# DeltaNet attention and a PReLU feed-forward on one NeuronCore: the triangular systems of the first two chunks solved by factors, and more weight staging

## The chip, the cores and the metric

The kernel runs on one core of one Trainium2 chip. A core has five engines with instruction streams of their own: TensorE (PE: matrix products, with a separate step that loads the stationary operand, PEld), VectorE (DVE), ScalarE (ACT), GpSimd (POOL) and SyncE (SP), which here only issues DMAs. Products land in PSUM, eight banks of 128 x 512 float32; VectorE and ScalarE read them from there. The metric is device microseconds of one launch; the time before is the median of three runs, 659.95 us (657.76 to 663.39).

## The reference

q, k and v are (4, 8, 768, 48): four batches, eight heads, 768 positions, head dimension 48. Attention is the delta rule, a recurrence over positions, and its output goes through a two-layer feed-forward of width 2048:

```python
k_n = k / (np.linalg.norm(k, axis=-1, keepdims=True) + 1e-06)
for t in range(S):
    y[:, :, t] = q[:, :, t] @ state                       # per batch and head
    v_old = k_n[:, :, t] @ state
    state = state + bt * outer(k_n[:, :, t], v[:, :, t] - v_old)
x = y.transpose(0, 2, 1, 3).reshape(B * S, H * D)         # 3072 x 384
h = x @ w_in                                              # 384 x 2048
out = (np.maximum(h, 0) + alpha * np.minimum(h, 0)) @ w_out   # 2048 x 384
```

(The einsums of the recurrence are written as products here.) The weights arrive as 64-bit floats and the kernel turns them into float32 with integer operations.

## The kernel before

**Chunks and steps.** The sequence is cut into 12 chunks of 64 positions. One step handles one chunk of two batches with their eight heads, so there are 24 steps, and step n is chunk n // 2 and batch pair n % 2. Inside a chunk the recurrence becomes a linear system with a unit lower triangular matrix of 64 x 64 per batch and head, I + A, where A holds the weighted products of keys (`grams`). A step solves it for the values (`through_state` makes the right side, `solve` multiplies by the inverse), then makes its outputs (`outputs`) and the next state (`next_state`), and turns its output for the feed-forward (`to_ffn`). The two 64-row halves of the partitions hold the two batches.

**The inverses.** Four steps share one elimination. `keep` and `gather` collect the diagonal blocks of 32 x 32, `turn_in` transposes them so that each partition holds one block as a row of numbers, `eliminate` runs a column elimination on VectorE, and `back` transposes the result twice, into `inverse` and into `turned`. The 32-wide inverses become 64-wide ones by two products (`between`, `products`, `copied`), and `placing` puts them where `solve` reads them. For the first four steps (the first two chunks) `eliminate_small` inverts blocks of 16 x 16 only (14 columns instead of 30) and `cross` makes the 32-wide inverses from them by two rounds of products of 32 rows, with `edges` masking one operand.

**The order.** Every engine's order is written by hand: the order of the calls in the source is the order of the instructions. The setup makes keys and grams of steps 0 to 3 on a period of about 2 us. Then `busy(BUSY)` gives TensorE products of no use while VectorE eliminates. `first_chunk` carries steps 0 and 1 from the inverses to `to_ffn`, with keys of the next steps and some `busy` products between. `second_pair` does steps 2 and 3; there `alongside(p, c)` weaves p products of the first layer for chunk 0 (`ffn_in(0)`, 48 products) and c halves of weight conversions between the attention's bursts. After it come `ffn_in(1)` with the rest of the conversions, then a long regular loop (lines 1776 to 1835) in which each step's attention is woven into feed-forward products by `stretch`.

**Weights.** `weights` stages w_in in 12 pieces of 512 KB and w_out in 16 of 384 KB. A piece is loaded by SyncE into spare room, ScalarE makes two of the parts (`begin`, lines 226 and 227), and VectorE joins them in two instructions (lines 236 and 241), one at each step of `conv_in`. Before the change eight w_in pieces have room of their own; the last four reuse staging space, so their loads wait on SyncE's queue until the piece before has been joined.

**Waits.** SyncE issues in program order, so a load whose buffer is still in use holds every load behind it. VectorE, ScalarE and GpSimd also run in order. PSUM for attention is three pairs of banks taken in turn (`ps_big`); the first layer uses two further banks in turn (`ps_ffn`), each emptied by an ScalarE (line 944) and two VectorE instructions (line 946).

Of the kernel before, what the change touches and what calls it, by code (L numbers as in the profile page):

```python
# [32 lines left out]
C = 64  # L33
HB = 32
# [9 lines left out]
def kernel(  # L44
# [138 lines left out]
    def weights(pieces, stages, ids, done, limit=None):  # L183
# [48 lines left out]
        def finish():  # L232
            for i in range(count):
                begin(min(i + 2, max(ahead[0], i + 1)))
                lo, _, dst = halves(i)
                nc.vector.tensor_scalar(
# [4 lines left out]
                nc.vector.tensor_tensor(  # L241
# [20 lines left out]
    above = const.tile([128, C], FP32, name="above")  # L262
    minus = const.tile([128, C], FP32, name="minus")
    for t in range(2):
        nc.gpsimd.tensor_copy(out=above[half(t)], in_=upper[half(t), half(t)])
# [21 lines left out]


# [149 lines left out]
    def grams(n, p=None):  # L438
# [9 lines left out]
        def weighted(dst, cols):  # L448
# [5 lines left out]

        return [
            lambda: weighted(gather(n), slice(0, HB)),
            lambda: weighted(right[n % EARLY][:, 1:], slice(HB, C)),
            lambda: keep(n),
        ]
# [52 lines left out]
    def turn_in(m):  # L512
# [4 lines left out]
            lambda x: block[m][:, :, x].rearrange("b r c -> b c r"),  # L517
# [30 lines left out]
    def back(m, late=False):  # L548

        r = block[m]  # L550
        turned[m] = work.tile([128, NJ * H, HB], FP32, name="turned", bufs=1)
        transposed = turns(
            lambda x: turned[m][:, :, x].rearrange("c b r -> c r b"), lambda x: r[:, x]
        )
        for _ in range(PIECES // 2 if late else PIECES):
            next(transposed)
            yield
# [5 lines left out]
        yield from transposed  # L563
# [5 lines left out]
    def eliminate_small(m):  # L569
# [22 lines left out]
        yield from back(m, True)  # L592

    def edges(m, dst):

        src = same[m].rearrange("p j h c -> p (j h) c")[:, :, LB:HB]
        nc.scalar.mul(dst[:, :, LB:HB], src, first_of)
# [4 lines left out]
    def cross(m, bs, edge, half_way, aside=None):  # L602


        def let(b, every):
            if aside is not None and b % every == every - 1:
                aside()

        n = bs.stop - bs.start
        p = ps_one()[:, 0 : n * LB].rearrange("p (b i) -> p b i", i=LB)  # L610
        for b in range(n):
            for i in range(4):
                nc.tensor.matmul(
                    p[quad(i), b], edge[quad(i), bs.start + b],
                    turned[m][quad(i), bs.start + b, 0:LB],
                )
            let(b, 4)
        nc.scalar.copy(half_way[:, bs, 0:LB], p)
        yield
        p = ps_big()[:, :, 0 : n * LB].rearrange("p w (b i) -> p w b i", i=LB)  # L620
        for b in range(n):
# [1248 lines left out]
```

## Time and profile before

| | |
|---|---|
| runs shown | 657.76, 663.39, 659.95 us; median 659.95 |
| span of the profiled execution | 663.9 us, the only time recorded for it |
| TensorE busy, of the span | 645.3 us, 97% |
| VectorE, ScalarE, GpSimd busy | 490.0, 262.5, 93.9 us |
| mean granted TensorE clock | 0.984 |
| bytes moved by DMA | 37.72 MB |
| first first-layer product (line 934) | at 50.77 us |
| second call of the first layer begins | at 97.58 us |

The profile is one execution. Its page gives the busy time of each engine, the span in forty slices with busy tenths, the groups of instructions by source line, and the DMA queues. The trace behind it can be asked for a stretch of time: a window table (busy time and granted clock by stage) or a timeline (instructions merged, with what ended the idle time ahead of them). A busy TensorE is not TensorE at its peak; its instructions overlap, and at a granted clock of 0.50 the same products take longer and still count as busy.

### The profile page before, as it was taken

To read this page: it belongs to the slowest core of one execution; us is meant where nothing else is said; L and a number is where in the kernel's file an instruction comes from. 1 tells how busy PE (TensorE), PEld (TensorE's weight loads), DVE (VectorE), ACT (ScalarE), POOL (GpSimd) and SP (SyncE) were. 2 spreads that over 40 slices of the span, in tenths; PEclk is the share of its full clock that TensorE was granted. 3 is DMA by queue.
4 is the path that set the end of the run, shared out by engine and by line. 5 is a ranking of instruction groups with operands and counts; after the bars stand their busy time and mean duration, and the time that the engine had idled before them with its cause. 6 is when DMAs were issued, how large, how long until landed. Compare 5 with 4: busy or idle time off the path is not lost.

```text
span 663.9 us, 22107 instructions
## 1 busy us (share of the span) xinstructions
PE 645.3 (97%) x9543; PEld 567.4 (85%) x9543; DVE 490.0 (74%) x1179; ACT 262.5 (40%) x616; POOL 93.9 (14%) x201
## 2 busy tenths in 40 slices
PE   5898999999999999999999999999999999999997
PEld 4567788656788988998998998998999999999997
DVE  4965598987899869748859758858968658568283
ACT  5457656424555343243343233232235235042140
POOL 6000211110010100001000000000035044053260
PEclk9969799999999999999999999999999999999999
DMA  7946556211342122122112112112111210100000
GB/s 118 287 93 161 121 174 161 72 34 29 62 86 50 24 52 49 26 49 49 27 38 37 25 39 38 26 38 38 26 40 36 37 35 5 28 12 2 24 1 25
DMA packets 111154, 37.72 MB, mean 57 GB/s; under 512 B 104224, under 2 KB 107440, under 8 KB 111056
## 3 DMA queue, kind: packets, MB, share of 16 engines
q1 hardware_dynamic: 109184, 35.81, 24.6%
q8 instruction: 75, 1.23, 0.8%
q10 hardware_dynamic: 1872, 0.49, 0.4%
q14 instruction: 23, 0.19, 0.1%
HBM read 31.56 MB, written 4.72 MB: 55 GB/s over the span
## 4 chain that ended last, share of the span: by engine, by line
PE 86%; DVE 6%; SPq 2%; ACT 2%; DMA 2%; issue 2%; ACTq 0%; DVEq 0%
PE p_ffn L934 20%; PE p_ffn L999 17%; PE p_more L1251 8%; PE p_ffn L977 5%; PE p_more L1167 4%; PE p_ffn L1157 3%; PE p_ffn L1251 3%; PE p_pair L691 3%; PE p_pair L392 2%; PE p_ffn L1162 2%; PE p_pair L766 2%; PE p_pair L791 2%; PE p_pair L804 2%; PE p_pair L1398 2%; PE p_pair L444 1%
## 5 line engine op out<-in xcount | busy, mean ns | idle before, releaser
L934 PE MATMUL p_ffn<-xt,w_in 128*128 128x256 f32 x768 | 179.4, 388 | 0.8 <-DVE act L946 0.5
L934 PEld LDWEIGHTS p_ffn<-xt,w_in 128*128 128x128 f32 x768 | 144.2, 192 | 22.3 <-issue 2.0
L946 DVE SCALAR_TENSOR_TENSOR act<-act,al_t,p_ffn 128x256 f32<-128x256 f32 x112 | 48.6, 475 | 27.8 <-ACT act L944 27.7
L944 ACT ACTIVATE act<-p_ffn 128x512 f32<-128x512 f32 x56 | 33.3, 595 | 84.2 <-PE p_ffn L934 84.0
L542 DVE TENSOR_TENSOR block<-block,prod 128x30 f32<-128x30 f32 (+9 forms) x150 | 49.8, 332 | 5.1
L1191 POOL TENSOR_TENSOR k_t<-k_t 128x128 f32<-128x128 f32 (+1 forms) x48 | 29.6, 616 | 167.3 <-ACT k_t L1186 164.8
L536 DVE TENSOR_TENSOR prod<-block 128x30 f32<-128x30 f32 (+9 forms) x150 | 48.7, 325 | 1.4
L999 PE MATMUL p_ffn<-w_out,act 128*128 128x192 f32 x288 | 49.6, 328 | 0.0
L381 POOL TENSOR_TENSOR beta_t<-beta_t,rec 128x8 f32<-128x8 f32 x24 | 6.4, 265 | 288.0 <-DVE rec L375 269.3
L999 PEld LDWEIGHTS p_ffn<-w_out,act 128*128 128x128 f32 x288 | 46.5, 190 | 0.3
L845 ACT COPY xt<-p_pair 128x384 f32<-128x384 f32 x22 | 10.4, 479 | 91.1 <-PE p_pair L843 77.3
L1191 POOL TENSOR_TENSOR block<-block 128x128 f32<-128x128 f32 (+1 forms) x48 | 28.0, 583 | 16.7 <-ACT block L1186 14.2
L1157 PE MATMUL p_ffn<-xt,w_in 128*128 128x256 f32 x96 | 28.7, 381 | 0.5 <-DVE o_sb L1019 0.5
L707 ACT COPY inv<-p_pair 32x256 f32<-32x256 f32 x46 | 16.6, 362 | 26.1 <-DVE u L795 24.1
L776 DVE TENSOR_TENSOR r<-v_raw,p_pair 64x192 f32<-64x192 f32 (+1 forms) x66 | 23.2, 352 | 2.3 <-PE p_pair L766 1.2
L795 DVE TENSOR_TENSOR u<-p_pair,wgt 128x384 f32<-128x384 f32 x24 | 13.2, 555 | 14.0 <-PE p_pair L691 14.0
L1019 DVE TENSOR_TENSOR o_sb<-u,p_ffn 128x192 f32<-128x192 f32 x24 | 7.9, 350 | 20.5 <-PE p_ffn L999 20.0
L1205 DVE SCALAR_TENSOR_TENSOR act<-block,al_t,act 128x256 f32<-128x256 f32 x32 | 19.1, 638 | 5.2 <-ACT block L1201 5.1
L977 PE MATMUL p_ffn<-w_out,act 128*128 128x384 f32 x64 | 21.7, 490 | 0.3 <-DVE more L946 0.3
L1251 PE MATMUL p_more<-w_out,act 128*128 128x192 f32 x128 | 21.9, 329 | 0.0
L755 ACT COPY y<-p_pair 128x384 f32<-128x384 f32 x22 | 10.4, 479 | 28.7 <-PE p_pair L751 27.1
L1186 ACT COPY k_t<-p_more 128x512 f32<-128x512 f32 x16 | 9.4, 586 | 31.3 <-PE p_more L1167 26.7
(226 smaller groups left out, 1412.6 us busy)
## 6 DMA issues: line engine op xcount, KB each, us to landing
w_out<-in_moe_w_in_dram SPq DMA_DIRECT2D x10, 512.0 KB, 5.3
qp<-in_q_dram SPq DMA_DIRECT2D x48, 96.0 KB, 2.7
v_raw<-in_v_dram SPq DMA_DIRECT2D x48, 96.0 KB, 3.1
kl<-in_k_dram SPq DMA_DIRECT2D x96, 48.0 KB, 2.5
out_dram<-o_sb SPq DMA_DIRECT2D x90, 48.0 KB, 1.6
space_out<-in_moe_w_out_dram SPq DMA_DIRECT2D x11, 384.0 KB, 4.5
ke<-in_k_dram SPq DMA_DIRECT2D x43, 96.0 KB, 3.4
w_out<-in_moe_w_out_dram SPq DMA_DIRECT2D x5, 384.0 KB, 6.8
```

The lines of the kernel that those rows point to most:

```text
L536: nc.vector.tensor_tensor(out=prod, in0=r[:, 0:j, j : j + 1].to_broadcast([128, j, n]), in1=r[:, j : j + 1, j + 1 : HB].to_broadcast([128, ...
L542: nc.vector.tensor_tensor(out=r[:, 0:j, j + 1 : HB], in0=r[:, 0:j, j + 1 : HB], in1=prod, op=ALU.add)
L776: nc.vector.tensor_tensor(out=r[to, a], in0=v_in[to, a], in1=p[own, a, :, 0:D], op=ALU.subtract)
L934: nc.tensor.matmul(p_h[:, i], w_in[:, t, (f + i) * 128 : (f + i + 1) * 128], xt[:, t], start=(t == 0), stop=(t == KT - 1),)
L944: nc.scalar.activation(g, p_h, ACT.Relu, scale=-1.0)
L946: nc.vector.scalar_tensor_tensor(out=g[:, i], in0=g[:, i], scalar=al_t[:, f + i : f + i + 1], in1=p_h[:, i], op0=ALU.mult, op1=ALU.add,)
L977: nc.tensor.matmul(p_o[u], gs[f // 2][:, f % 2, u * 128 : (u + 1) * 128], w_out[:, f], start=(f == 0), stop=(f == FT - 1),)
L999: nc.tensor.matmul(p, x(i), w(i), start=(i == 0), stop=(i == FP - 1))
L1157: nc.tensor.matmul(p[:, f * 256 : f * 256 + 256], w(2, f), xt[:, 2], start=True, stop=False)
L1167: nc.tensor.matmul(q[:, j], a, b, start=True, stop=True)
L1191: nc.gpsimd.tensor_tensor(out=dst, in0=a, in1=b, op=ALU.add)
L1251: nc.tensor.matmul(p, x(i), w(i), start=(i == 0), stop=(i == FP - 1))
```

## The change

Steps 0 to 3 no longer get 64-wide inverses. Write the matrix as D + E, where D holds its four 16 x 16 diagonal blocks and E what lies outside them. With M = -inverse(D) E, the solution is (I + M)(I + M^2) inverse(D) times the right side, exactly, since M^4 is zero. So `matrices` makes M and its transpose by 32 products of 64 x 64, `squared_matrix` makes M^2, and three bursts of 16 products each (`first_factor`, `second_factor`, `third_factor`) carry the values through. `cross`, `edges`, `between_both` and the use of `solve` in these steps go, and `back` no longer transposes a second time for them. The masked outside blocks (`outside`, into `beyond`) and the placed 16-wide inverses (`place_small`, into `own_inverse`) are made by ScalarE and VectorE. The values of steps 0 and 1 are scaled by GpSimd (`scale_first`).

The w_in staging takes three more spaces, in tiles that are idle then, so eleven pieces are loaded without reuse; the load calls and the numbers of conversions woven into each stretch are rearranged. In `second_pair` the load of v for step 3 and its scaling stand next to each other, and the bursts follow a new order. In the late loop the pieces put off in every fourth step are woven from 0.1 of a stretch on instead of 0.5.

```diff
@@ setup
-    above = const.tile([128, C], FP32, name="above")
+    eye = const.tile([128, C], FP32, name="eye")
...
+    below = const.tile([128, 2], FP32, name="below")
+    nc.gpsimd.tensor_tensor(out=below, in0=which, in1=first_of.to_broadcast([128, 2]), op=ALU.mult)
...
@@ def grams(n, p=None): (steps 0 to 3)
             lambda: weighted(gather(n), slice(0, HB)),
-            lambda: weighted(right[n % EARLY][:, 1:], slice(HB, C)),
+            lambda: weighted(right[n][:, 1:], slice(HB, C)),
             lambda: keep(n),
+            lambda: weighted(beyond[n][:, :, 0:HB], slice(0, HB)),
         ]
@@
-    def cross(m, bs, edge, half_way, aside=None):
...
+    def outside(n, part):
+        x, left, last = beyond[n], beyond[n][:, :, 0:HB], right[n][:, 1:, 0:LB]
+        if part == 0:
+            src = left if n < 2 else same[0][:, n]
+            nc.scalar.mul(left[:, :, 0:LB], src[:, :, 0:LB], below[:, 0:1])
+            nc.scalar.mul(left[:, :, LB:HB], src[:, :, LB:HB], which[:, 1:2])
+        else:
+            nc.scalar.mul(x[:, :, HB : HB + LB], last, below[:, 1:2])
...
+    def place_small(n, by_vector):
+        for i in range(2):
+            whole_block(own_inverse[n], inverse[0][:, n * H : n * H + H], i, by_vector)
@@ def through_state(n, p=None, p_y=None):
+            *([lambda: weigh_rest_side(n)] if n < NJ else []),
             *asked,
             lambda: masked(n, p[:, :, :, D : D + C]),
         ]
+    def weigh_rest_side(n):
+        w = stats[n][1][:, 0:2, :, None].to_broadcast([128, 2, G, D])
+        nc.vector.tensor_tensor(out=rhs_[n], in0=rhs_[n], in1=w, op=ALU.mult)
+
+    def scale_first(n):
+        c, bp = steps[n]
+        nv[n] = v_raw.pop(n)
+        nc.gpsimd.tensor_tensor(
+            out=nv[n], in0=nv[n], in1=beta_t[:, c, bp, :, None].to_broadcast([128, H, D]),
+            op=ALU.mult,
+        )
+        rhs_[n] = by_parity(nv[n])
+
+    def crossing(out, x, y, back):
+        for g, a, t in quarters():
+            rows, own = (half(t ^ a), half(t)) if back else (half(t), half(t ^ a))
+            nc.tensor.matmul(out[own, a, g], x[rows, a, g], y[rows, a, g])
+
+    def matrices(n, p=None):
+        p = ps_big() if p is None else p
+        one, other = (region(p[:, :, i * G * C : (i + 1) * G * C], G * C, g=G) for i in range(2))
+        x, y = heads(own_inverse[n]), heads(beyond[n])
+        crossing(one, x, y, False)
+        crossing(other, y, x, False)
+        m, m_t, plus, _ = (heads(z) for z in power_space[n])
+        def add():
+            nc.vector.tensor_tensor(
+                out=plus, in0=other, in1=eye[:, None, None, :].to_broadcast([128, 2, G, C]),
+                op=ALU.add,
+            )
+        return [lambda: nc.scalar.copy(m_t, other), add, lambda: nc.scalar.copy(m, one)]
+
+    def squared_matrix(n, p):
+        p = region(p, G * C, g=G)
+        m, m_t, _, plus = (heads(z) for z in power_space[n])
+        crossing(p, m, m_t, True)
+        return [lambda: nc.vector.tensor_tensor(
+            out=plus, in0=p, in1=eye[:, None, None, :].to_broadcast([128, 2, G, C]), op=ALU.add
+        )]
+
+    def first_factor(n, p, engine=nc.scalar):
+        p = region(p, G * D, g=G)
+        crossing(p, heads(own_inverse[n]), rhs_[n], False)
+        return [lambda: copy_by(engine, by_parity(nv[n]), p)]
...
+    def third_factor(n, p, engine=nc.scalar):
+        p = region(p, G * D, g=G)
+        crossing(p, heads(power_space[n][3]), rhs_[n], False)
+        us[n] = work.tile([128, 2, G, D], FP32, name="u")
+        return [lambda: copy_by(engine, us[n], p)]
@@ def first_chunk(mask, convert):
-        middle = cross(
-            0, slice(0, 2 * H), edge, half_way, lambda: pause and busy(next(waits, 0), pause[0])
-        )
...
-        now(between_both(both, True))
...
+        place_small(0, True)
+        place_small(1, False)
         for i in both:
             mask(i)
+        p, z = [ps_big(), ps_big()], ps_big()
+        for i in both:
+            soon.append(matrices(i, p[i]) + first_factor(i, side(z, i), nc.vector))
+        for i in both:
+            now(soon[i])
+        convert(4)
+        for i in both:
+            x = ps_big()
+            soon.append(second_factor(i, x[:, :, 0 : G * D]))
+            soon[i] += squared_matrix(i, x[:, :, G * C : 2 * G * C])
+        now(soon[0])
+        now(soon[1])
         keys = flipped(NJ, ps_ffn())
+        soon = [third_factor(0, side(z, 0))]
+        now(keys)
+        soon.append(third_factor(1, side(z, 1), nc.vector))
+        now(soon[0])
+        now(soon[1])
+        for i in both:
+            now(outputs(i))
+        for i in range(2, NJ):
+            place_small(i, i == 2)
+        keys = flipped(NJ + 1, ps_one())
+        for i in both:
+            to_ffn(i, ps_ffn())
+        now(keys)
+        convert(4)
...
@@ staging and loads
-    ids = [*range(n_in + 2), 0, 2, 1, 3]
-    fetch_in, begin_in, conv_in = weights(pieces, stages, ids, in_done, n_in + 2)
+    words = more.rearrange("p i s e -> p (i s e)").bitcast(U32)
+    stages += [words[:, i * n : (i + 1) * n] for i in range(2)]
+    stages += [sums.rearrange("p i s e -> p (i s e)").bitcast(U32)[:, 2 * n : 3 * n]]
+    ids = [*range(n_in + 5), 0]
+    fetch_in, begin_in, conv_in = weights(pieces, stages, ids, in_done, n_in + 5)
...
     fetch_in(n_in + 2)
+    load_late(1)
+    load_v(2)
+    for i in range(2):
+        scale_first(i)
     for n in range(1, NJ):
         load_early(n + NKE)
-    edges(0, edge)
+    fetch_in(n_in + 5)
...
     busy(BUSY)
     begin_in(3)
+    for n in range(2, NJ):
+        outside(n, 1)
+    begin_in(5)
     for _ in eliminate_small(0):
@@ def second_pair():
         now(next_state(0))
         load_late(2)
         alongside(2, 1)
         now(next_state(1))
         fetch_in(n_in + 6)
+        alongside(4, 3)
+        load_late(3)
         load_v(3)
         for i in both:
             scale_v(i)
...
         now(pieces)
+        alongside(4, 3)
+        now(matrices(n))
+        squares(x + 2)
+        now(weigh(x))
+        alongside(2, 2)
+        now(matrices(m))
...
+        alongside(4, 3)
+        burst(first_factor, G * D)
+        now(weigh(x + 1))
+        fetch_out(3)
+        alongside(5, 4)
+        burst(second_factor, G * D)
+        alongside(2, 1)
+        burst(squared_matrix, G * C)
...
+        alongside(5, 3)
+        burst(third_factor, G * D)
+        now(grams(x))
...
@@ late loop
-                fill[2], blocks, share[2], later, *after, *extra[2], soon=0.1 if n >= LATE else 0.5
+                fill[2], blocks, share[2], later, *after, *extra[2], soon=0.1 if n >= LATE or ends else 0.5
```

## The prediction

> **What bounds the kernel now.** I read the page's busy times and forty slices first, then a table of the span by stage, then two-microsecond windows of the worst stages, then the timeline there.
>
> ```profile
> PE 645.3 (97%) x9543; PEld 567.4 (85%) x9543; DVE 490.0 (74%) x1179; ACT 262.5 (40%) x616; POOL 93.9 (14%) x201
> PE   5898999999999999999999999999999999999997
> ```
>
> TensorE is the bound nearly everywhere. The stages below are: warm-up beside the elimination; steps 0 and 1 (the first chunk) up to the first feed-forward product; steps 2 and 3 up to the second call of the first layer; its conversions and elimination; the rest. Columns: window, length, busy time and (in brackets) instructions of each engine, granted clock, DMA share, GB/s.
>
> ```profile
> 20.60:29.10 8.50, 8.50 (x28) 3.71 (x28) 7.65 (x26) 4.31 (x9) 0.00 (x0) 1.00 1.09 364
> 29.10:50.80 21.70, 18.23 (x635) 13.45 (x635) 15.56 (x37) 9.92 (x21) 0.00 (x0) 0.76 0.50 104
> 50.80:97.60 46.80, 44.33 (x1053) 36.23 (x1050) 32.32 (x80) 30.83 (x71) 7.17 (x17) 0.89 0.59 152
> 97.60:125.00 27.40, 26.90 (x184) 21.70 (x183) 24.92 (x73) 17.07 (x39) 3.84 (x10) 1.00 0.54 133
> 125.00:660.00 535.00, 533.69 (x7440) 481.39 (x7439) 398.45 (x934) 187.85 (x446) 71.87 (x132) 1.00 0.17 34
> ```
>
> From 125 to 660 us TensorE idles 1.3 us at full clock, so what the change wins or loses before 97.6 us arrives at the end unchanged, and the end can't win more. All that is open lies in the 68.5 us of the second and third line: 5.9 us idle, clock 0.76 and 0.89. Closer:
>
> ```profile
> 30.00:32.00 2.00, 0.10 (x10) 0.00 (x0) 2.00 (x6) 0.00 (x0) 0.00 (x0) 1.00 0.34 58
> 36.00:38.00 2.00, 1.55 (x97) 1.41 (x97) 0.16 (x1) 0.77 (x2) 0.00 (x0) 0.50 0.59 104
> 64.00:66.00 2.00, 0.58 (x32) 0.55 (x32) 0.23 (x2) 0.73 (x2) 0.00 (x0) 0.80 0.61 119
> 70.00:72.00 2.00, 2.00 (x71) 1.29 (x69) 1.47 (x4) 0.60 (x1) 0.74 (x2) 0.50 0.90 233
> 72.00:74.00 2.00, 2.00 (x36) 1.72 (x35) 1.08 (x4) 1.88 (x5) 0.00 (x0) 0.50 0.79 227
> ```
>
> Twice TensorE empties inside the cross products, and a stretch at half clock follows each time. The timeline shows why it empties, and gives the prices used below:
>
> ```profile
> 32.24 0.37 PE L613 MATMUL p_pair<-turned,sums 32*32 32x16 f32 x22 [2.15 <-issue]
> 65.42 0.23 PE L628 MATMUL p_pair<-inverse,act 32*32 32x16 f32 x1 [2.19 <-issue]
> 51.83 0.68 PE L820 MATMUL p_pair<-u,kl 64*64 64x48 f32 x32
> 78.09 0.69 PE L444 MATMUL p_pair<-k_t 48*64 48x64 f32 x32
> 97.58 7.76 PE L934 MATMUL p_ffn<-xt,w_in 128*128 128x256 f32 x34
> 38.55 9.51 SPq L210 DMA_DIRECT2D w_out<-in_moe_w_in_dram  x2
> ```
>
> Both stalls wait on no engine ("issue"). The instruction queue q8 brings 16 KB at a time (1.23 MB in 75 packets, so some 127 product-and-load pairs each), and packets started at 29.28 and 62.80 us and took 1.57 and 1.33: 106 tiny products ran off in 1.07 us, faster than the next packet came. The last row shows SyncE's queue held 9.5 us because a weight piece waits for its staging space.
>
> **First chunk.** A call in the source is two matmul rows (16 calls, x32). Removed before the first feed-forward product: 64+96 calls of cross, 64 of between_both, 32 of solve = 256, the fillers behind the warm-up (2.75 times 512 columns, 1.12 us for one), the second transposition on VectorE. Added: per step 32 calls (matrices) and 16 each for first, second, squared, third = 192. They are 64x64 products: by L444 0.69 us, by L820 0.68 us per 16 calls at full clock, or 21 ns a row, so 127 pairs take 2.7 us against a packet that comes some 3.0 us after it starts to be missed (29.28 to 32.24): I charge one stall of 0.3 us where 2.15 was.
>
> The start doesn't move: the warm-up ends at 29.1 in both. Elimination ends at 26.6 now; one gather on GpSimd (0.85 us) leaves ahead of turn_in and two masked ACT copies come in, net -0.5; four inverse transposes of 0.54 and two L656 (0.31) give 28.8. Two VectorE rows (0.42) per early step are added in setup, inside a 2.1 us period where VectorE holds 1.5; scale_first on GpSimd (0.78 for 256 columns, so 1.2 each) is over by 18 us and unused until 30.5. Both cost nothing; uncovered, 0.4 and 2.4 us. ScalarE converts two more pieces ahead (2.7 us) before place_small(1): 29.4, plus two L660 rows of 0.45, 30.3, needed at 31.2. On SyncE the k load of step 4 falls behind six others of 0.65 us: it lands near 34, its flip is due at 36.4. Both are covered by a microsecond or two; without that they cost what they are late.
>
> From 29.1: matrices and first factor of both steps 2 x (1.38+0.68)+0.3 = 33.6. VectorE: masks, add 0.69 (as L464), copies to 34.25, then two conversions (0.42+0.69 each) to 36.45, so that the queued add of M squared for step 0 ends at 37.15, for step 1 at 37.85. Third factors to 38.65, ACT and VectorE copies 0.5 to 39.25, outputs to 40.05, copy to 40.65, flip and to_ffn to 41.6, VectorE copy of xt (three of some 0.25; bounds 0.15 and 0.48, from small rows and the whole copy L845) 42.35, next_state, first product at **43.0** against 50.8. If the clock halves at 34.5 as now, each later burst costs 1.1 for 0.69 (L444 at 71.94) and the same chain ends at **47.3**. Nearest rows point both ways: the 32-wide bursts at 34 to 38 us fell to 0.50, the 64-wide ones at 46 to 48 us filled the engine and the clock came back to 0.96 in the next window. After the change TensorE is almost without gaps between 31 and 42 us. I take 44.8: **-6.0**, range -3.5 to -7.8.
>
> Three more pieces are staged: 1.5 MB at the 400 GB/s of 18 to 26 us is 3.9 us of DMA, queued behind k and v loads at 35 to 39.5 us; needed from about 60. Cover is ample, and SyncE's 9.5 us wait goes.
>
> **Second pair.** TensorE loses 160+64+32 calls (1.4+2.0+1.6+1.3 = 6.3 us at full clock) and gains 2.75+3 x 1.15+1.38 = 7.6: +1.2. The 2.2 us stall and the half clock of 65 to 75 us (4.6 us) had that cause. VectorE gets more: four conversion halves (+2.2), two weighings 1.1, four adds 2.8, less the cross adds 1.7 and u 1.0 = +3.3, to 35.6 us. **Added wait:** scale_v(3) now follows load_v(3) at once. SyncE issues eight k loads (0.65 each), a weight piece and two v loads after next_state(0), some 9 us, landing 1.5 later; VectorE arrives about 2.7 us before. Behind it queue the subtractions, masks, adds and conversions of steps 2 and 3; TensorE has 20 us of products but is held where a bank waits for masked (about 0.7 us), at the first-layer evacuation L946 (1.2) and the third factor (1.2). Bounds of the wait: 0 (v there early) and 6 us (the longest kl group, 4.75, plus landing); 2.7 is from the nearest issue rows. Laid out row by row in program order the stage takes 45.0 against 46.8: **-1.8**, and the layout ignores small delays, so I keep +0.5 back. What is late next is VectorE: 38.3 of 45 us.
>
> The pieces' earlier start in the late loop (0.1 instead of 0.5) moves VectorE and GpSimd work inside a stage with 1.3 us of idle: 0, bounds -1 and +1.
>
> Sum: -6.0-1.8+0.5 = -7.3 against the profiled execution's 663.9: 656.6. That execution is 3.9 above the median of the runs, 659.95, which becomes about **652.6**; I predict 652.5. 1% is 6.6 us, about what a measurement of this kernel can tell from no change.
>
> The Trainium skill, "TensorE: Matmul & The Clock Gate", section "Part 1: The HAM clock gate", has the clock return after one busy window of some 3.4 us, windows running free of the kernel. The rows from 66 to 74 us speak against it (busy 2.00 of 2.00 at 0.50 for 8 us), those at 46 to 48 for it; the free phase agrees with runs 5.6 us apart. By it the first rival holds.
>
> **Rivals.**
> - Full clock throughout: 43.0 and 45.0, -9.6, **650.4**. For it: 64-wide products without gaps. Against: clock 0.76 today with fillers.
> - Half clock from 34.5 to 47, second pair as laid out: -4.3-0.5, **655**. For it: the windows of before.
> - The gain is given back to VectorE: the v wait at 6 us and conversions in front of evacuations keep the pair's end at 95 to 97: 0 to -3, **658.5**. For it: VectorE already 24.9 of 27.4 us busy right after.
> - Slower: fillers are gone, first-chunk gaps halve the clock at 34.5, and the v wait breaks the windows so it returns only at 75 as it did after 65. Then 28 us from 47.3 do 14 us of work, the other 27 follow, 3 of stalls: 106 instead of 97.6, +8.6, **668.5**. It decides where half clock outlasts 65 us. Against: feed-forward products of 128 columns and rows lie between.
> - The change doesn't do its work (bursts starve on instructions again, 2 us four times): **660**.
>
> **Numbers.** Forecast (650.5 to 653.3) 0.26, full clock 0.20, half clock early 0.20, given back 0.16, slower 0.14, starving 0.04. Faster by over 1%: 0.46; within: 0.40; slower: 0.14. Range 646 to 664: below the full-clock case by a good run, above to the given-back case and run spread; out are most of the slower case and 0.05 below.
>
> **What would show it.** First L934 product near 43 to 47, second ffn_in start near 88 to 93, no "issue" wait over 1 us before 97, SyncE not held 9 us, a VectorE idle of 2 to 3 us released by the v load, PE busy to the end. Wrong if clock 0.50 is granted past 55 us, if VectorE is idle much longer, or if a first-layer product waits for a piece's conversion.

## The result: 1.1% slower

| | before | after |
|---|---|---|
| median of the runs | 661.06 us (4 runs) | 668.22 us (4 runs, 667.22 to 669.21) |
| ratio after to before | | 1.0111, 95% interval 1.0077 to 1.0145 |
| span of the profiled execution | 663.9 us | 666.9 us |
| TensorE busy, mean granted clock | 645.3 us, 0.984 | 640.3 us, 0.984 |
| first first-layer product | 50.77 us | 51.38 us |
| second call of the first layer begins | 97.58 us | 100.45 us |
| first second-layer product | 121.97 us | 126.26 us |

Predicted were 652.5 us and a range of 646 to 664. The sign is wrong. The changed kernel's profiled execution is a typical one (668.62 us timed for a span of 666.9). A span is thus 1.7 us shorter than the time; for the 663.9 of the kernel before that makes an estimated 665.6, above all four of its runs. The pair of traces therefore shows 3.0 of the 7.2 us between the medians; a second trace of the kernel before, below, shows more.

The page of the changed kernel, busy times and the slices of TensorE and its clock:

```profile
PE 640.3 (96%) x9279; PEld 567.4 (85%) x9279; DVE 490.6 (74%) x1175; ACT 266.4 (40%) x619; POOL 94.8 (14%) x210
...
PE   5778799999999999999999999999999999999997
...
PEclk9969999999999999999999999999999999999999
```

264 products fewer and 5.0 us less of TensorE work, and a later end. The second to the fifth slice fell from 8989 to 7787. By stage, with the bounds used for the kernel before (window, length, busy time and instructions of TensorE, its weight loads, VectorE, ScalarE, GpSimd, granted clock, DMA share, GB/s):

```profile
20.60:29.10 8.50, 6.93 (x28) 3.06 (x20) 7.69 (x27) 8.34 (x18) 0.00 (x0) 1.00 1.07 375
29.10:50.80 21.70, 16.54 (x482) 15.18 (x486) 10.58 (x26) 8.60 (x19) 0.00 (x0) 0.62 0.59 128
50.80:97.60 46.80, 40.41 (x903) 32.90 (x898) 34.42 (x79) 28.86 (x61) 4.80 (x14) 0.96 0.55 141
97.60:125.00 27.40, 25.75 (x208) 21.26 (x207) 24.43 (x71) 15.26 (x32) 5.26 (x12) 1.00 0.48 114
125.00:660.00 535.00, 534.24 (x7441) 481.12 (x7440) 401.16 (x940) 192.05 (x455) 71.47 (x132) 1.00 0.17 34
```

TensorE idles 13.1 us between 20.6 and 97.6 us, where the kernel before idled 5.9. The waits behind that, summed over 27 to 125 us (engine, line, what it waited for; total, times, longest):

```profile
PE p_pair L776 <- issue: 2.9, 2, 1.5
PE p_pair L776 <- DVE inv L627: 2.5, 1, 2.5
PE p_pair L776 <- DVE a_t L483: 2.2, 1, 2.2
PE p_pair L776 <- ACT v_raw L810: 1.9, 1, 1.9
PE p_pair L776 <- ACT space_out L227: 1.3, 1, 1.3
PE p_ffn L991 <- ACT w_out L226: 1.2, 1, 1.2
```

Line 776 is `crossing`, the products of the new solution. "Issue" is time in which TensorE waited for nothing that the profile shows; below it turns out to be waiting for instructions. There are still two such waits; the 2.5 us ahead of the first of its products and the waits for VectorE and ScalarE are new. Where they stand, from the timeline (start, length, engine and queue, what, and in brackets the idle time before and its end):

```profile
30.07 0.69 PE L776 MATMUL p_pair<-sums,inv 64*64 64x64 f32 x32 [2.54 <-DVE inv L627]
...
33.89 0.81 PE L776 MATMUL p_pair<-sums,inv 64*64 64x64 f32 x20 [1.37 <-issue]
...
35.03 2.09 SPq L210 DMA_DIRECT2D more<-in_moe_w_in_dram  x2
...
37.17 0.43 SPq L210 DMA_DIRECT2D sums<-in_moe_w_in_dram  x1
...
44.06 0.67 PE L776 MATMUL p_pair<-r,act 64*64 64x48 f32 x28 [1.50 <-issue]
...
50.38 1.75 SPq L137 DMA_DIRECT2D ke<-in_k_dram  x2
...
58.32 1.27 SPq L137 DMA_DIRECT2D v_raw<-in_v_dram  x2
...
62.71 0.56 DVE L710 TENSOR_TENSOR v_raw<-v_raw,norm 128x384 f32<-128x384 f32 x1 [4.42 <-DMA v_raw<-in_v_dram]
...
65.51 1.13 PE L776 MATMUL p_pair<-sums,diag 64*64 64x64 f32 x32 [2.23 <-DVE a_t L483]
```

The added wait for v of step 3 is there: VectorE stands 4.42 us in `scale_v(3)`, and what is queued behind it (the mask of line 483) holds TensorE. Ahead of that load SyncE had stood 9.1 us, until ScalarE's line 363 let go of the buffer of a k load at 50.38, and then issued for 8 us what stands before v in its queue. The three added weight pieces (lines with `more` and `sums`) go out at 35.0 to 37.6 us, between the two issue waits.

The difference by marks, against the two traces of the kernel before:

| stretch | before | before, again | after | after less each |
|---|---|---|---|---|
| to the first first-layer product | 50.77 | 51.29 | 51.38 | +0.6, +0.1 |
| from there to the second call | 46.81 | 44.55 | 49.07 | +2.3, +4.5 |
| from there to the first second-layer product | 24.39 | 23.99 | 25.81 | +1.4, +1.8 |
| from there to the end of the span | 541.9 | 541.6 | 540.6 | -1.3, -0.9 |

The first chunk gains nothing; the second pair loses; 1.4 to 1.8 us are lost right behind it and about 1 us comes back in the rest.

### The profile page after: what moved, and what is told of

It is laid out like the page before. It is cut to its first block, busy times and chain, and to the rows that moved or that the text cites. A ratio compares the mean times of both kernels' runs of the same rounds, so it can differ in the third digit from the quotient of the medians.

```text
span 666.9 us, 21587 instructions
## 1 busy us (share of the span) xinstructions
PE 640.3 (96%) x9279; PEld 567.4 (85%) x9279; DVE 490.6 (74%) x1175; ACT 266.4 (40%) x619; POOL 94.8 (14%) x210
## 4 chain that ended last, share of the span: by engine, by line
PE 83%; DVE 9%; ACT 3%; issue 2%; DMA 1%; SPq 1%; POOL 0%; DVEq 0%; POOLq 0%; ACTq 0%
PE p_ffn L991 21%; PE p_ffn L1056 17%; PE p_more L1308 8%; PE p_ffn L1034 5%; PE p_more L1224 4%; PE p_ffn L1214 3%; PE p_ffn L1308 3%; PE p_ffn L1219 2%; PE p_pair L673 2%; PE p_pair L404 2%; PE p_pair L733 2%; PE p_pair L849 2%; PE p_pair L456 2%; PE p_pair L776 2%; PE p_pair L836 2%
## 5 line engine op out<-in xcount | busy, mean ns | idle before, releaser
L991 PEld LDWEIGHTS p_ffn<-xt,w_in 128*128 128x128 f32 x768 | 142.6, 190 | 24.5 <-issue 2.2
L555 DVE TENSOR_TENSOR prod<-block 128x30 f32<-128x30 f32 (+9 forms) x150 | 48.9, 326 | 1.4
L1056 PEld LDWEIGHTS p_ffn<-w_out,act 128*128 128x128 f32 x288 | 46.5, 190 | 0.3
L685 ACT COPY inv<-p_pair 32x256 f32<-32x256 f32 x40 | 14.5, 361 | 24.9 <-DVE u L840 24.2
L733 PE MATMUL p_pair<-beside,k_t 48*64 48x112 f32 x704 | 21.3, 259 | 0.2 <-ACT beside L432 0.2
```

The source lines that it names most:

```text
L555: nc.vector.tensor_tensor(out=prod, in0=r[:, 0:j, j : j + 1].to_broadcast([128, j, n]), in1=r[:, j : j + 1, j + 1 : HB].to_broadcast([128, ...
L733: nc.tensor.matmul(p[half(t ^ a), a, g], k_t[n][dims(a), g, half(t)], beside[bp][dims(a), t, g])
L991: nc.tensor.matmul(p_h[:, i], w_in[:, t, (f + i) * 128 : (f + i + 1) * 128], xt[:, t], start=(t == 0), stop=(t == KT - 1),)
L1056: nc.tensor.matmul(p, x(i), w(i), start=(i == 0), stop=(i == FP - 1))
```

## The experiments

The theory after the first trace of each kernel: the arithmetic is as cheap as worked out, and what it saves is lost in waits that the change adds or leaves: the v load behind the k loads, the start of the new solution, and instructions that come too late. The rival: more work on VectorE and ScalarE, or the half clock, sets the end of the second pair, whatever is done to single waits. All ratios are to the kernel before, on the same chip.

**The kernel before, again**, for the noise.

> The kernel before, once more, for a second trace of it and for the size of the noise. The time was 661.06 us by its median, but its first profiled execution (span 663.9) lies at the slow end of its runs (657.8 to 663.4). Expectation: 661 within 3 us of itself, ratio 1.000 within 0.004. If the second stretch at half clock (65 to 75 us) is chance, this trace has it shorter or not at all, and the third stage (50.8 to 97.6 us, 46.8 us long) is 2 to 5 us shorter; if it is built in, the trace repeats it.

Measured: 663.28 us, ratio 1.0011 (0.9981 to 1.0042). Its trace, span 661.4, has the same two issue waits (2.4 and 1.9 us). Half clock was granted at 31.9 to 42.1, 45.5 to 48.9 and 66.0 to 69.4 us, where the first trace has 34.5 to 41.3, 44.7 to 48.1 and 65.2 to 75.4. With 3.4 us of it in the second pair the pair took 44.6 us, with 10.2 us it took 46.8: nearly all of the 2.5 us between the two spans.

**The v load early.**

```diff
@@ second_pair
+        load_v(3)
         now(next_state(0))
         load_late(2)
...
         load_late(3)
-        load_v(3)
         for i in both:
             scale_v(i)
```

> The changed kernel with one line moved: the load of v for step 3 is issued ahead of next_state(0) in the second pair, not right before its scaling. In the changed kernel VectorE idles 4.42 us for it, TensorE 2.2 us behind VectorE, and 3.4 us at half clock follow. Theory 'added waits': the wait goes and 3 to 5 us come back, 663 to 665 against 668.2. Rival 'VectorE and ScalarE are full in the second pair anyway': the same work queues a little later, and less than 1 us comes back, 667 to 668.

Measured: 664.65 us, ratio 1.0017 (0.9992 to 1.0043). Against the changed kernel's 1.0111 (1.0085 in its repeat, below) that is 0.7 to 0.9%, 4.5 to 6 us. TensorE's longest waits in this kernel, 27 to 125 us:

```profile
PE p_pair L776 <- issue: 5.1, 3, 2.4
PE p_pair L776 <- ACT v_raw L810: 1.5, 1, 1.5
PE p_pair L776 <- ACT space_out L227: 1.3, 1, 1.3
```

And its second pair in the window table:

```profile
51.93:96.94 45.01, 41.41 (x925) 33.81 (x921) 34.54 (x80) 29.06 (x62) 5.56 (x16) 1.00 0.59 151
```

The wait for the mask of line 483 is gone, no half clock follows in the pair, and it takes 45.0 us. That is to the tenth what the prediction laid out, but with no wait for v, where the prediction had 2.7 us of it on VectorE. VectorE's and ScalarE's work is the same, so it is not their load that made the pair long. The first product came no earlier (51.93).

**Products of no use until the solution starts.**

```diff
-    BUSY = 7.5
+    BUSY = 9.5
```

> The changed kernel with the warm-up products beside the elimination lengthened from 7.5 to 9.5 (times 512 columns), so that they reach to about 29.3 us where the clock is already full at 20.8 us, and to about 31 where it is not. In the changed kernel TensorE idles 2.5 us ahead of the first new product and the clock is at half from 31.0 to 41.2 us. Theory 'the gap drops the clock': the first-chunk products up to 41 run at full clock, 2 to 4 us come back, 664 to 666. Rival 'the gaps between the new bursts drop it anyway': nothing comes back, 668, or 669 where the fillers end late.

Measured: 667.65 us, ratio 1.0084 (1.0052 to 1.0117): 0.3% under the changed kernel's first ratio, and the same as that of its repeat (1.0085), so no gain that can be told. In its trace, the fastest of its six runs, the first product comes at 47.87 us, 3.5 us earlier, and the second call starts at 97.86, 2.6 earlier; the waits of the pair (this kernel's waits of TensorE, 27 to 125 us) are still there:

```profile
PE p_pair L776 <- issue: 3.7, 2, 3.2
PE p_ffn L991 <- ACT more L227: 2.1, 1, 2.1
PE p_pair L776 <- DVE a_t L483: 1.8, 1, 1.8
```

SyncE starts again earlier here too, at 47.98 us, and the load of v moves with it:

```profile
55.45 1.27 SPq L137 DMA_DIRECT2D v_raw<-in_v_dram  x2
```

**The staging alone**, in the kernel before.

```diff
-    ids = [*range(n_in + 2), 0, 2, 1, 3]
+    ids = [*range(n_in + 5), 0]
...
     for i in range(2):
         load_q(i + 2)
+    fetch_in(n_in + 5)
     mask = queries()
```

> The kernel before with the staging part of the change alone: eleven pieces of the first-layer weights have room of their own and are loaded before the first chunk; SyncE no longer stands 9.5 us for a staging space. Nothing else moves. Theory 'staging is harmless and idle gain': 661 within 2 us, since no engine waited for those loads in the kernel before. Rival 'the extra 1.5 MB in front delays the k and q loads behind it or slows instruction fetches': 2 to 4 us slower, which would be a third to a half of the 7 us that the whole change lost.

Measured: 664.81 us, ratio 1.0032 (1.0002 to 1.0062). With the old solution the three pieces win nothing; whether they cost something, the interval leaves open (0 to 4 us, so both answers of the expectation fit). That SyncE no longer stands 9.5 us for a staging space was worth nothing.

**Both repairs.** The v load early and 9.5 in place of 7.5.

> The changed kernel with both repairs that helped alone: the load of v for step 3 issued ahead of next_state(0), and products of no use for 9.5 instead of 7.5 times 512 columns, so that TensorE is busy until the first M. Theory (the two losses are separate): the first pair ends as in the run with the longer filler, first-layer product near 47.9, the second pair takes the 45.0 us that it took with the early v, so the second call of the first layer starts near 93 and the time is 3 to 5 us under the run with early v alone, ratio to the kernel before 0.994 to 0.997. Rival A (what is won early is lost in the second pair, whatever v does, since first-layer conversions and ScalarE copies set its end): second call at 96 to 98, ratio 1.000 to 1.004. Rival B (the half clock, whose windows run by themselves, eats part of it): 0.997 to 1.000, with 0.50 granted for 7 us between 55 and 95.

Measured: 663.33 us, ratio 1.0001 (0.9979 to 1.0023). The second pair takes 44.6 us as the theory has it, but the first product is at 50.62, not at the expected 47.9. The reason stands in its timeline:

```profile
36.12 0.62 PE L776 MATMUL p_pair<-act 64*64 64x64 f32 x26 [0.86 <-issue]
...
42.84 1.11 PE L776 MATMUL p_pair<-r,act 64*64 64x48 f32 x32 [3.87 <-issue]
```

and in its DMA view of 34 to 43 us (queue, packets, MB, share of the 16 engines; then issues, KB each, median us to landing):

```profile
q1 hardware_dynamic: 3811, 2.20, 100.6%
q8 instruction: 1, 0.02, 0.6%
...
more<-in_moe_w_in_dram SPq DMA_DIRECT2D x2, 512.0 KB, 5.2
sums<-in_moe_w_in_dram SPq DMA_DIRECT2D x1, 512.0 KB, 7.9
qp<-in_q_dram SPq DMA_DIRECT2D x4, 96.0 KB, 7.2
```

TensorE waited 3.87 us for nothing but instructions, in a stretch in which the added weight pieces and the q loads filled all DMA engines, and in which one packet of instructions (16 KB) was moved.

**Products of no use between the bursts.** On top of both repairs, three products of 512 columns after the first factor of step 0 and three ahead of the third factor of step 1.

```diff
             soon.append(matrices(i, p[i]) + first_factor(i, side(z, i), nc.vector))
+            if i == 0:
+                busy(3, ps_ffn())
...
         now(keys)
+        busy(3, ps_ffn())
         soon.append(third_factor(1, side(z, 1), nc.vector))
```

> The kernel of the run with both repairs and, in the first chunk, three products of no use (512 columns each, 1.28 us at full clock) after the first factor of step 0 and three more ahead of the third factor of step 1. Theory (the two issue waits are TensorE waiting for a 16 KB packet of instructions that comes some 3 us after its start, and the packets follow each other by 3.3 us at best): the fillers lie inside these waits, the issue waits fall by 1 to 1.3 us each, and the first first-layer product comes no later than 0.5 us after that of the run without them; ratio to the kernel before within 0.2% of that run. Rival (the waits have another cause, a fixed delay after an instruction): the fillers come on top, 2.6 us, first product 2 to 2.6 us later, 0.3 to 0.4% slower. If the fillers also keep the clock at 1.00 between 31 and 45, 1 to 3 us faster.

Measured: 666.55 us, ratio 1.0062 (1.0037 to 1.0088): 0.6% slower than without them. The rows:

```profile
32.47 2.84 PE L1455 MATMUL p_ffn<-kl,ident 128*128 128x512 f32 x6
...
44.89 0.44 PE L776 MATMUL p_pair<-r,act 64*64 64x48 f32 x6 [2.90 <-issue]
45.26 4.37 PE L1455 MATMUL p_ffn<-kl,ident 128*128 128x512 f32 x6
```

The expectation had the price wrong: three such products are six rows and 2.84 us at full clock, 4.37 mostly at half, not 1.28. The first group takes the issue wait that stood there; the second lies behind the wait it was to fill, not inside it, and comes on top. It does not tell the two theories apart, though it shows that the second wait stays 2.9 us when everything ahead of it is shifted.

**Two conversion halves later.** On top of both repairs.

```diff
@@ second_pair
-        alongside(4, 3)
+        alongside(4, 2)
         burst(first_factor, G * D)
...
-        alongside(2, 1)
+        alongside(2, 0)
         burst(squared_matrix, G * C)
...
-        alongside(5, 3)
+        alongside(5, 4)
         burst(outputs, G * D)
...
-        alongside(5, 3)
+        alongside(5, 4)
         for i in both:
             to_ffn(i)
```

> The kernel of the run with both repairs and two conversion halves of the second pair moved: one from ahead of the first factors and one from ahead of the squared M to the stretches ahead of outputs and of to_ffn. Theory (ScalarE's and VectorE's conversions stand ahead of the copies that TensorE waits for: 1.5 us for v_raw and 1.3 us at the third factor in the run with early v): these two waits fall to under 0.7 us each, the second call starts 1.5 to 2.5 us earlier, 0.2 to 0.4% faster than without the move. Rival (VectorE and ScalarE are the bound there, and what is moved comes back later): the waits go but others of the same sum appear before 125 us, 0 to 0.1%.

Measured: 663.21 us, ratio 1.0004 (0.9983 to 1.0026), the same as without. The wait for the copies of line 810 fell from 0.8 to 0.5 us and that at the third factors (1.3) is gone, but the pair takes 44.9 us as against 44.6. These waits are not what the pair's end hangs on.

**All four together** (early v, 9.5, products between the bursts, conversions later).

> All together: early v, fillers to the start, fillers in the bursts, two conversions later. If all the theories hold: first first-layer product near 48, second call near 91 to 92, ratio to the kernel before 0.990 to 0.994. If VectorE and ScalarE bound the second pair: second call near 94 to 96, ratio 0.996 to 1.000.

Measured: 667.31 us, ratio 1.0068 (1.0042 to 1.0093): the products between the bursts cost the same 0.6% here, first product 54.24.

**When the packets came.** The packets of instructions are in the trace's DMA records. Where TensorE stops for instructions in the first chunk of the changed kernel and its variants, it is close to the 345th, 472nd or 599th product, though not at all three in every trace: one packet holds about 127 pairs of load and product. The table gives, for the packet that brings the products from the 599th on, the time from passing the boundary before it to the packet's start, and how busy the DMA engines were in that time; then the same for the next packet, when no weights are loaded.

| kernel | from 599: start after, DMA share | from 726: start after, DMA share |
|---|---|---|
| changed | 3.3 us, full | 1.05 us, 0.44 |
| early v | 4.25 us, 0.91 | 1.2 us, 0.01 |
| both repairs | 4.4 us, full | 1.55 us, 0.23 |
| both, fillers in bursts | 4.2 us, full | 1.1 us, 0.03 |
| both, conversions later | 3.7 us, 0.96 | 1.1 us, 0.19 |

From the packet's start to TensorE's next product it takes another 2.3 to 3.0 us. The two columns differ in more than the weights, and a full DMA share alone does not fix the delay: from the 980th product on, the packets of the changed kernel and its variants start 1.4 to 3.4 us after their boundary at shares of 0.85 to 1.12. So the next runs move the weights.

**The added pieces behind the bursts.** On top of both repairs.

```diff
-    fetch_in, begin_in, conv_in = weights(pieces, stages, ids, in_done, n_in + 5)
+    fetch_in, begin_in, conv_in = weights(pieces, stages, ids, in_done, n_in + 2)
...
-    fetch_in(n_in + 5)
     slopes()
...
@@ second_pair
         load_v(3)
+        fetch_in(n_in + 5)
         now(next_state(0))
```

> The kernel with early v and fillers to the start, and the three added weight pieces loaded behind the load of v for step 3 (they start near 52 us) instead of at 34 to 36 us. Theory (instruction packets queue behind weight pieces on the 16 DMA engines): in the run without this move the packet that TensorE needed after its 599th product started 4.4 us after the previous boundary was passed, with the DMA engines full, while packets beside sparse traffic started after 1.1 to 1.5; now it starts after 1 to 2 us, the longest issue wait before 50 us falls from 3.9 to under 1.5 us, the first first-layer product comes at 46.5 to 48.5 (50.6), and the ratio to the kernel before is 0.994 to 0.998. Rival A (the packet is slow whatever the weights do; the small-row loads of k and q or the fetch itself set it): issue wait still 3 us or more, ratio 0.999 to 1.002. Rival B (pieces at 52 us collide with the packets of the second pair or come late for their conversions): first product early, second call not, issue or ScalarE waits over 1.5 us between 55 and 75.

Measured: 660.99 us, ratio 0.9974 (0.9948 to 1.0000). The timeline of this kernel:

```profile
35.68 0.62 PE L776 MATMUL p_pair<-act 64*64 64x64 f32 x26 [1.14 <-issue]
...
40.48 1.10 PE L776 MATMUL p_pair<-r,act 64*64 64x48 f32 x32 [2.00 <-issue]
...
47.83 1.13 PE L991 MATMUL p_ffn<-xt,w_in 128*128 128x256 f32 x4
```

Its DMA view of the same 34 to 43 us:

```profile
q1 hardware_dynamic: 2909, 0.54, 33.5%
q8 instruction: 2, 0.03, 1.5%
...
qp<-in_q_dram SPq DMA_DIRECT2D x4, 96.0 KB, 3.2
```

The packet from the 599th product starts after 2.3 us instead of 4.4, the wait is 2.0 instead of 3.87, the q loads land in 3.2 us instead of 7.2, and the first product is 2.8 us earlier. The next two kernels move the pieces too: with them moved the packet starts after 2.3, 2.0 and 1.2 us, and in the eight traces of the changed kernel and its variants with the pieces at 34 to 38 us after 3.3 to 4.4. That the pieces delay the packet is shown. 2.0 us of wait is more than expected; that the q loads stand in front too was not tested. Rival B's collision is not borne out: with the pieces at 50 to 52 us the packet from the 980th product starts 3.0 us after its boundary, and 3.1 us without them. Its sign, an issue wait over 1.5 us, is there by a hair, 1.6 us at 60 us, where the kernel with the pieces early has 1.3. The pair takes 45.8 us instead of 44.6, with 3.4 us of half clock in it.

**The same move alone**, in the changed kernel, with the pieces at the start of `second_pair`.

> The changed kernel with nothing but this move: the three added weight pieces are loaded at the start of the second pair. Theory (packets behind weight pieces cost the first chunk its gain): issue waits before 50 us fall from 2.9 to about 1.5 us, first product at 49 to 50, 1.5 to 2 us faster than the changed kernel (ratio to the kernel before 1.007 to 1.009 where that has 1.011); the v wait stays. Rival (staging is innocent, as it was beside the old solution): same as the changed kernel, 1.010 to 1.012; or slower, as the v load then stands behind 1.5 MB more: 1.013 to 1.016.

Measured: 668.48 us, ratio 1.0088 (1.0058 to 1.0118); the changed kernel beside it, next, has 1.0085. No gain, and yet in its timeline the first product comes at 46.54 us, 4.4 earlier than in the trace beside it:

```profile
46.41 2.00 SPq L137 DMA_DIRECT2D ke<-in_k_dram  x2
...
46.54 1.13 PE L991 MATMUL p_ffn<-xt,w_in 128*128 128x256 f32 x4
...
58.58 1.27 SPq L137 DMA_DIRECT2D v_raw<-in_v_dram  x2
...
62.51 0.56 DVE L710 TENSOR_TENSOR v_raw<-v_raw,norm 128x384 f32<-128x384 f32 x1 [8.22 <-DMA v_raw<-in_v_dram]
...
65.31 1.13 PE L776 MATMUL p_pair<-sums,diag 64*64 64x64 f32 x32 [5.33 <-DVE a_t L483]
```

VectorE waits 8.2 us for v instead of 4.4 and goes on at 62.5, when it went on in the changed kernel (62.7); the second call starts at 100.28 (100.45). SyncE starts again 4.0 us earlier than in the first trace of the changed kernel, at 46.41, but the three pieces now stand ahead of v, and with the k loads slower behind them v is issued at 58.58, as late as before (58.32). This is what the rival's second half feared, only that it costs the whole gain and no more. With the longer warm-up nothing was put ahead of v, and v came 2.9 us earlier. So the time at which v is there sets the end of the pair, and what stands before it in the queue sets that time. Nor are the 4.4 us all the pieces' doing: the stop at the 345th product, which comes before they are issued, was 2.0 us in the trace beside it and is gone here, as in every trace in which the packet for it starts at 23 to 24 us instead of 31. What moves that packet is open.

**The changed kernel, again.**

> The changed kernel itself, beside the other runs: ratio to the kernel before 1.008 to 1.014 as when it was first shown; first product 50 to 52, issue waits of 1 to 1.5 us twice before 50 us. It says how far the runs of one kernel lie apart, so that the run with the staging moved can be read.

Measured: 668.53 us, ratio 1.0085 (1.0055 to 1.0116), with v waited for 4.0 us and TensorE held 2.2 at line 483.

**Both repairs, pieces behind the bursts, conversions later.**

> Early v, fillers to the start, staging behind the bursts, and the two conversion halves later. If the theory on packets holds: first product at 46.5 to 48.5, second call at 91 to 93, ratio to the kernel before 0.992 to 0.997, faster than the kernel before for the first time. If not: as with the first, second and fourth of these alone, 0.998 to 1.003.

Measured: 661.13 us, ratio 0.9992 (0.9961 to 1.0023). First product 46.47, second call 92.14: the trace is at the expected marks, the median is not. The traced run, 660.38 us, is a little below that median. Against the same kernel with the pieces early, the issue waits before 50 us fall from 4.3 to 1.2 us and the first product comes 2.5 us earlier. Only the kernel without the conversions' move is under the kernel before, by 0.3%, with an interval that touches 1; the two repaired kernels differ by less than their intervals.

**Time and clock over the runs.** Every run lists its mean granted clock. Fitted by a straight line (± is two standard errors):

| kernel | runs | mean clock | us per 0.01 of clock lost | us at full clock |
|---|---|---|---|---|
| before | 87 | 0.988 | 3.1 ± 0.9 | 658.7 ± 1.2 |
| changed | 10 | 0.988 | 1.0 ± 1.8 | 667.1 ± 2.3 |
| both repairs, pieces behind the bursts | 12 | 0.995 | 3.4 ± 1.6 | 658.7 ± 0.9 |

By these lines the changed kernel is about 8 us slower at full clock and about 6 us at 0.988, where its runs lie. Its slope is too uncertain (-0.8 to 2.8) to say whether its time depends less on the clock. The repaired kernel is at full clock no faster than the kernel before; its 0.3% would then be in the higher clock, 0.995 against 0.988, at some 3 us per 0.01. That is a fit over few runs on several chips, not a proof.

## Why the prediction was wrong, step by step

**First chunk, -6.0: measured +0.6 (+0.1 against the second trace).** The step that failed is the stall: "I charge one stall of 0.3 us where 2.15 was". Two waits of 1.4 and 1.5 us were there, in the repeat 4.6 in three. The reckoning (127 pairs run in 2.7 us, a packet takes 3.0) counted from the packet's start; it left out the 1.0 us or more from the boundary to that start even with no weights beside it, and that packets share the DMA engines with loads. The three pieces of weights that the change adds went out at 35 to 37.6 us, and the packet for the second wait started 3.3 us after the boundary. The first wait came before the pieces. Moving them, on top of both repairs, brings the first product from 50.6 to 47.8, and with the conversions later from 49.0 to 46.5. That is about the slower of the prediction's two cases, 43.0 at full clock and 47.3 at half. An estimate bears it out: 47.3, with the start 1.0 us later (30.07, below) and 2.6 us more of stalls, makes 50.9 of the measured 51.38, so the chain of bursts itself was laid out about right.

"The start doesn't move: the warm-up ends at 29.1 in both" was a smaller error: the warm-up ended at 27.5, its 16 rows having taken 6.71 us instead of 8.51, which differs from trace to trace (8.59 in the one with the early v), and VectorE's masked copies (line 627) of the inverse ended at 29.9 us, where 28.8 had been worked out, and the first product of the solution stood at 30.07. `turn_in` began 0.5 us later than before (16.33 against 15.80) instead of 0.5 earlier: `keep(3)` waited 0.43 us for ScalarE's masked copies (line 616), and its copy took 0.78 us where 0.28 was the time before. TensorE was idle for 2.5 us just ahead of the first product, and half clock followed from 31.0 to 41.2 us. The gap alone does not explain the loss: with the early v it was 0.3 us, the solution started at 29.92, and the first first-layer product came at 51.93 all the same. How much of the loss is the clock's, the runs don't settle, since its phase differs in each.

**Second pair, -1.8: measured +2.3 (+4.5 against the second trace).** The added wait was found, placed and bounded (0 to 6 us), but sized at 2.7 us where 4.4 and 4.0 were measured, and its effect on TensorE was taken as mostly covered, where TensorE stood 2.2 us. The mis-sized term is the landing: SyncE issued for 9.2 us where "some 9" were reckoned, but v was there 3.1 us after the last issue, not 1.5. The early v load wins back 4.5 to 6 us of the median and brings the pair to 45.0 us. The second step that failed is the gain itself. "The 2.2 us stall and the half clock of 65 to 75 us (4.6 us) had that cause" took the half clock as built in; the second trace of the kernel before has the same kind of stall (1.9 us), only 3.4 us of half clock behind it, and a pair of 44.55 us. So even with v there, 45.0 us is no gain over that trace: the 2.3 us between the two traces of the kernel before are more than the whole -1.8. And the run with the pieces moved shows what a load in the wrong place does: 4.4 us won before the pair, 8.2 us waited, the same end.

**Staging, "Cover is ample".** Right for the pieces themselves, which no conversion waited long for. Wrong in that transfers were costed only by when they land, not by what else has to pass the same engines.

**Behind the pair** the prediction had nothing; 1.4 to 1.8 us are lost between the second call and the first second-layer product. TensorE waits there for 1.2 us behind a weight conversion on ScalarE, and this stays in all variants. **The sum** takes the profiled execution as 3.9 us above the median, but sets a span beside a time; with the 1.7 us between the two it is 5.6 above, by the same estimate as at the head of the result. The forecast takes this excess off and counts the long half clock, which is likely part of it, as a gain as well: some of it is taken off twice.

**The late loop** was put at 0, with bounds of 1: in the traces the stretch from there to the end is 0.9 to 1.3 us shorter. It was not undone alone, so what part the earlier pieces have in it is open.

**The rivals.** The slower one (668.5, chance 0.14) gave nearly the measured time, but not its mechanism: half clock was to last from 34.5 to 75 us; it was granted in two stretches up to 51.5 us and came back for 3.4 us only, at 65.1. Its own terms (47.3, 28, 27 and 3) add up to 105.3 us, not 106. The point from which it was to decide, half clock outlasting 65 us, was not what decided. "Given back to VectorE", with the v wait as its cause, is the nearest to what happened, though it stopped at 0 to -3. That the bursts "starve on instructions again" had 0.04 and was part of it. Each was priced alone; that together they make the sign is the reading that fits the runs, of which the v load alone is shown to be worth 4.5 to 6 us.

**What was to show it.** TensorE stayed busy to the end, as foretold. SyncE was no longer held for a staging space, but it stood 9.1 us at the next k load instead. Issue waits over 1 us and the pair's end at 100 miss what was named; half clock past 55 us, VectorE idle much longer than 2 to 3 us and first-layer products behind a piece's conversion (0.8 and 1.2 us) are the signs named for a wrong prediction.

## What to carry to other kernels

Where a stage waits for a load, time won ahead of it is worth nothing unless the load is issued earlier: look first at what stands before it in its queue and what releases that queue, and move the load (one line, some 5 us here). Read more than one trace before counting a stretch of half clock as a gain. Long bursts of small products, as here 127 in 2.7 us, use up instructions faster than they were seen to come, 3.3 us apart at best; weight loads that are not urgent belong outside such bursts. A DMA that "has time" still costs what is queued behind it, instruction fetch included.

## What was not expected of the hardware

**Instruction packets queue behind data.** Over the whole of the traces no two packets of 16 KB start less than 3.3 us apart. 127 products of 64 x 64 run off in an estimated 2.7 us (21 ns a row), so bursts outrun even undisturbed fetching; with three weight pieces on the DMA engines, a packet started 3.3 to 4.4 us after the boundary, and waits of up to 3.9 us came of it. The Trainium skill, "Runtime: NRT & Kernel Launch", section "Instruction fetch mechanics", calls the cost of crossing a 16 KiB block mostly hidden. The late loop agrees (TensorE idles 0.8 us in 535), these bursts do not.

**The clock's windows run by themselves.** The stretches at half clock last 3.4, 6.8 or 10.2 us and lie elsewhere in every trace of the same kernel. The Trainium skill, "TensorE: Matmul & The Clock Gate", section "Part 1: The HAM clock gate", states free-running windows of 3413 ns, which these lengths bear out. What the phase costs is seen in the kernel before: its second pair took 46.8 us with 10.2 us at half clock, and 44.6 with 3.4.
